# States times W_in for four chunks in one TensorE stretch, and the second softmax's read behind the next scores

## The chip, the cores and the metric

The kernel runs on one core of one Trainium2 chip. The metric is the device time of one execution in microseconds. It uses TensorE (PE) for all products, ScalarE (ACT) and VectorE (DVE) for everything element by element, and SyncE (SP) and ACT for issuing DMAs. GpSimd does almost nothing.

## The reference, cut to what matters

Two computations follow one another: an exchange between 512 tokens and 32 states in each of 8 heads and 8 batches, and a two-layer product with a piecewise quadratic activation on its result.

```python
B, H, S, Ns, D = (8, 8, 512, 32, 64)
scores = scale * np.matmul(x, state.transpose(0, 1, 3, 2))
a = softmax(scores)                        # over the 32 states
xread = np.matmul(a, state)                # tokens read the states
scores2 = scale * np.matmul(state, x.transpose(0, 1, 3, 2))
a2 = softmax(scores2)                      # over the 512 tokens
sread = np.matmul(a2, x)                   # states read the tokens
attn_out = np.concatenate([xread, sread], axis=2)
...
h = x @ w_in                               # x: attn_out as 4352 rows of 512; w_in: 512 x 2048
g = np.where(h >= 1, h, np.where(h <= -1, 0.0, (h + 1) ** 2 / 4))
return g @ w_out                           # w_out: 2048 x 512
```

All data are float32. The weights arrive as float64 and are turned into float32 on the chip.

## The kernel before, in words

**What is computed where.** The product of the attention weights with the states and then with W_in is reordered: for each batch b the states are multiplied with W_in first (`sw`), and the attention weights are multiplied with that. So the first layer is `h = sw^T x attention weights`, in place of `xread` and then `W_in`. W_in is cut into 8 chunks of 256 columns (c = 0 to 7), the hidden layer into 8 steps (j = 0 to 7) of 256 hidden units. Step (b, j) of batch b needs chunk j of `sw` for this batch.

Each float32 operand of the large products is split into a high part and a rest (`ath`/`atl` for the attention weights, `sw_..h`/`sw_..l` for `sw`, `gh`/`gl` for the activation, `wo` for W_out), and a product is three matmuls: high x high, rest x high, high x rest.

**A step (b, j)** does, in the code's order:

- `g1(b, j)`: 12 matmuls of 128x512 (lines 477 to 479), six into each of two banks called h. Then ACT takes Relu of each bank (`relu`, line 482), squares both (`square`, line 485), DVE takes minimum and maximum with the bank itself (`bound`, line 488: two operations, after which the two h banks are free), ACT makes the high part (`high`, line 497), DVE the rest (`low`, line 502).
- `g2` of the step before: 24 matmuls of 128x512 (lines 534 to 536), 8 pairs of three, into four banks called acc. In the last step of a batch they are ordered by output tile, and each finished tile is copied out by ACT (`store`, line 549) and written by a DMA that ACT issues.

So TensorE always has 24 matmuls of the step before to do while ACT and DVE turn h into g.

**Between g1 and g2** of a step stand the small products:

- `sw_make(b, c, 2)` (line 438), in every odd step for the next two steps: 16 matmuls (32 records of two passes each) of 64 rows, 32 columns and 256 elements, eight at a time on different parts of the array (line 417). They write the two banks called mm. ACT copies the high part (line 432), DVE subtracts for the rest (line 436).
- the `Attention` of batch b+1, as a generator of four pieces, one in each even step: `scores` (`sc`, line 253, 8 matmuls of 64 rows and 32 columns) with what the second softmax needs on DVE and ACT; the first softmax and the transposes of the second softmax's weights (`e2p`, line 333); the transposes back, the splitting, and the read `sr` of the second softmax (line 350, 32 matmuls of 128 rows and 32 columns) with its scaling `rs` on DVE (line 358); and the transpose of that read (`rt`, line 364), copied to `srT` by ACT.

`sc`, `e2p`, `sr`, `rt` and `sw` all use the same two mm banks, one after the other.

**What sets the order.** The first batch (b = 0) with all loading and conversion of weights is ordered by a planner (`Plan`) with costs; TensorE's and SP's order there is the written order. Batch 0's phase also holds scores, transposes, read and read's transpose of batch 1. From batch 1 on, the framework's scheduler takes the instructions in the code's order as their priority and moves some of them ahead on their own engine; buffers are tiles in rings, and a tile is free when its last reader is done. The last part, batch index 8, puts the 256 rows of `sread` of all batches through the two layers in four steps.

Of the kernel before, what the change touches and what calls it, by code (L numbers as in the profile page):

```python
# [8 lines left out]
F32 = mybir.dt.float32  # L9
F32R = mybir.dt.float32r  # L10
# [3 lines left out]
ALU = mybir.AluOpType  # L14
# [8 lines left out]
class Plan:  # L23
# [13 lines left out]
    def op(self, key, engine, cost, run, after=(), take=(), ends=()):  # L37

        after = list(after)
        prior = self.last.get(engine) if engine in ("PE", "SP") else None  # L40
        self.last[engine] = key
        self.ops[key] = [engine, cost, run, after, list(take), list(ends), prior]
# [95 lines left out]
def state_exchange_moe(  # L138
# [17 lines left out]
    nc = tc.nc  # L156
    B, P, NT, H, D = x.shape
    S = NT * P
    NS = 32
    DM = H * D  # L160
    NPR = H // 2
    CI = 256
# [3 lines left out]
    NJ = NF // 2  # L166
# [6 lines left out]
    work = ctx.enter_context(tc.tile_pool(name="work", bufs=2))  # L173
# [7 lines left out]
    def ps_h(name):  # L181
        return ps.tile([P, 512], F32, tag="h", bufs=2, name=name)

    def ps_mm(name):
        return ps.tile([P, 2, 512], F32, tag="mm", bufs=1, name=name)
# [3 lines left out]
    half = small.tile([P, 1], F32, name="half")  # L189
# [14 lines left out]
    sb = const.tile([P, B, NPR, NS], F32, name="sb")  # L204
    srT = const.tile([P, NPR, B, NS], F32, name="srT")
    w32 = [const.tile([P, NPR, CI], F32, name=f"w32_{c}") for c in range(NC)]
# [4 lines left out]
    loaded = {}  # L211
    att_of = {}

    def load_xt(b):
        xt = work.tile([P, 2, NPR, S // 2], F32, tag="xt", bufs=1, name=f"xt{b}")
        for i in range(2):
            nc.sync.dma_start(out=xt[:, i], in_=xt_in[b, i])
        return xt
# [6 lines left out]
    class Attention:  # L225
# [116 lines left out]
        def read2(self):  # L342
            b = self.b
            xn = loaded.pop(("xn", b))
            sr = self.sr = ps_mm(f"sr{b}")
            for q in range(2):
                for t in range(NT):
                    for pr in range(NPR):
                        c0 = t * P + pr * NS
                        nc.tensor.matmul(  # L350
                            sr[pr * NS:(pr + 1) * NS, q, :D], lhsT=self.e2[:, q, c0:c0 + NS],
                            rhs=xn[:, t, 2 * pr + q], start=t == 0, stop=t == NT - 1,
                        )

        def scale2(self):
            b = self.b
            self.rs = small.tile([P, 2, D], F32, tag="rs", name=f"rs{b}")
            nc.vector.tensor_tensor(
                out=self.rs, in0=self.sr[:, :, :D], in1=self.r2[:, :, None].broadcast_to([P, 2, D]), op=ALU.mult
            )  # L360

        def keep2(self):
# [7 lines left out]
                out=srT[:, :, self.b], in_=self.rt[:, 0, :P].rearrange("p (g n) -> p g n", n=NS)  # L370
            )

        def steps(self):
            self.scores()
            for q in range(2):
                self.turn(q)
            for q in range(2):
                self.top2(q)
            for q in range(2):
                self.exp2(q)  # L380
            yield
            for f in (self.top1, self.less1, self.exp1, self.sum1, self.inv1, self.norm1):
                for q in range(2):
                    f(q)
            self.turn2()
            self.keep_turned()
            yield
            for q in range(2):
                self.back(q)
                self.high1(q)  # L390
                self.rest(q)
            self.read2()
            self.scale2()
            yield
            self.keep2()
            self.keep()
            yield

    def split_tiles(name):
        hi = work.tile([P, 1024], F32R, tag="wh", name=f"{name}h")
        lo = work.tile([P, 1024], F32R, tag="wl", name=f"{name}l")
        return hi, lo

    chunk = {}
# [27 lines left out]
    def sw_low(b, c):  # L434
        pt, wh, wl = sw_of[b, c]
        nc.vector.tensor_tensor(out=wl, in0=pt, in1=wh.bitcast(F32), op=ALU.subtract)

    def sw_make(b, c, n):
        sw_product(b, c, n)
        sw_high(b, c)  # L440
        sw_low(b, c)

    def wi_split(c):
        wh, wl = (v.rearrange("p (k f) -> p k f", f=CI) for v in split_tiles(f"wj{c}"))
# [59 lines left out]
    def g1(b, j):  # L504
        hid = Hidden(b, j)
        for i in range(2):
            hid.product(i)
            hid.relu(i)
        hid.square()
        for i in range(2):  # L510
            hid.bound(i)
        hid.high()
        hid.low()

    def g2(b, j, half=None):
        n = n_of[b]
        per = S // n
        nt = n // P
        if b not in acc:
            acc[b] = [ps_acc(f"acc{b}_{t}") for t in range(nt)]  # L520
        gh, gl = gs[b, j]
        last = j == NJ // per - 1
        pairs = [(i, t) for i in range(2 * per) for t in range(nt)]
        if last:
            pairs.sort(key=lambda p: p[1])
        if half is not None:
            pairs = pairs[half * len(pairs) // 2:][:len(pairs) // 2]
        for i, t in pairs:
            f = 2 * per * j + i
            oh, ol = wo[f // 2][:, 0, f % 2], wo[f // 2][:, 1, f % 2]  # L530
            c0 = (i % per) * n + t * P
            lh, ll = (v[:, i // per, c0:c0 + P] for v in (gh, gl))
            a = acc[b][t]
            nc.tensor.matmul(a, lhsT=lh, rhs=oh, start=f == 0, stop=False)  # L534
            nc.tensor.matmul(a, lhsT=lh, rhs=ol, start=False, stop=False)  # L535
            nc.tensor.matmul(a, lhsT=ll, rhs=oh, start=False, stop=f == NF - 1)  # L536
            if last and i == 2 * per - 1:
                store(b, t)
# [74 lines left out]
    op = plan.op  # L613
# [25 lines left out]
    atts = {}  # L639
# [34 lines left out]
    def att_ops2(b):  # L674
        def m(name, *a):
            return lambda: getattr(atts[b], name)(*a)

        for q in range(2):
            k = (b, q)
            take = [("tmp" if b == 0 else "e2", ("e2", b))] if q == 0 else []  # L680
            op(("top2",) + k, "DVE", 0.8, m("top2", q), [("sc", b) if b else ("sc", b, 1)] + [("top2", b, 0)] * q, take=take)
            op(("exp2",) + k, "ACT", 0.66, m("exp2", q), [("top2",) + k], ends=[("sc", b)])
        op(("kept", b), "ACT", 0.95, m("keep_turned"), [("e2p", b)], ends=[("e2p", b)])
        op(("rs", b), "DVE", 0.25, m("scale2"), [("sr", b)], ends=[("sr", b)])
        op(("srT", b), "ACT", 0.3, m("keep"), [("rt", b)], ends=[("rt", b)])

    hid = {}

# [12 lines left out]
    def tensor(key, cost, f, after=(), take=(), ends=()):  # L701
        op(key, "PE", cost, f, after, take, ends)
# [24 lines left out]

    def g2_ops(b, j, half):
        k = (b, j)
        tensor(("g2", half) + k, 2.75, lambda: g2(b, j, half), [("gh",) + k, ("gl",) + k, ("wol", j), ("sc done", 0)],  # L730
               ends=[("g",) + k])


# [21 lines left out]
    for side in range(2):  # L755
        tensor(("sc", 0, side), 0.6, lambda side=side: att_start(0, side), [("dma", "xt", 0, side)],
               ends=[("xt", 0)])
# [6 lines left out]
                          take=[("mm", ("e2p", 0))]),  # L764
# [3 lines left out]
                          take=[("mm", ("sc", 1))], ends=[("xt", 1)]),  # L768
        3: lambda: tensor(("rt", 0), 0.3, lambda: atts[0].keep2(), [("rs", 0)], take=[("mm", ("rt", 0))]),
        4: lambda: tensor(("e2p", 1), 0.9, lambda: atts[1].turn2(), [("exp2", 1, 0), ("exp2", 1, 1)],  # L770
                          take=[("mm", ("e2p", 1))]),
        5: lambda: tensor(("sr", 1), 1.1, lambda: atts[1].read2(), [("kept", 1), ("dma", "xn", 1)],
                          take=[("mm", ("sr", 1))], ends=[("e2", 1), ("xn", 1)]),
        6: lambda: tensor(("rt", 1), 0.3, lambda: atts[1].keep2(), [("rs", 1)], take=[("mm", ("rt", 1))]),
    }
    for j in range(NJ):
        g1_ops(0, j)
# [18 lines left out]

    steps = [(b, j) for b in range(1, B + 1) for j in range(NJ if b < B else NJ // 2)]

    def prepare(b, j):
        if b < B:  # L800
            if j % 2 == 0:
                sw_make(b, j, 2)
        elif b == B:
            for c in (2 * j, 2 * j + 1):
                wi_split(c)

    for i, (b, j) in enumerate(steps):
        if j == 0:
            if b + 1 < B:
                loaded["xt", b + 1] = load_xt(b + 1)  # L810
                loaded["xn", b + 1] = load_xn(b + 1)
                att = Attention(b + 1).steps()
            elif b == B:
                sh, sl = (work.tile([P, NPR, B * NS], F32R, tag=t, name=f"s{t}") for t in ("ath", "atl"))
                src = srT.rearrange("p a b n -> p a (b n)")
                nc.vector.tensor_copy(sh, src)
                nc.vector.tensor_tensor(out=sl, in0=src, in1=sh.bitcast(F32), op=ALU.subtract)
                att_of[B] = (sh, sl)
        g1(b, j)
        if i + 1 < len(steps):  # L820
            prepare(*steps[i + 1])
        if b < B and j % 2 == 0:
            next(att, None)
        g2(*(steps[i - 1] if i else (0, NJ - 1)))
    g2(*steps[-1])


# [41 lines left out]
```

## Time and profile before

| what | value |
| --- | --- |
| median of 3 runs | 663.71 us (663.57 to 663.91) |
| span of the profiled execution, first to last instruction | 662.2 us |
| TensorE busy | 653.9 us, 4442 matmul records |
| VectorE busy | 340.3 us |
| ScalarE busy | 356.5 us |
| DMA | 43.65 MB, mean 66 GB/s |

The profile shows one execution by its span, the time between its first and last instruction; the device time of the same kernel is the median above, 1.5 us more than that span. In a timeline each row gives the start in us from the span's start, the duration, the engine, the line of the kernel, the operation, the tile written and those read, their shapes, how many instructions are merged in the row, and in brackets the idle time of the engine before it with what ended it. PE is TensorE's matmuls, PEld its weight loads. Matmuls overlap: a row's duration is not the time after which the next one starts, so on TensorE the distance between starts is what counts.

### The profile page before, as it was taken

The numbers are of one execution on the slowest core, as the hardware profiler recorded it, in microseconds if no ns is written. First come the engines' busy times: TensorE is split into PE (matmuls) and PEld (weight loads), VectorE is DVE, ScalarE is ACT, GpSimd is POOL, SyncE is SP. The second block draws the span as 40 slices with busy tenths as digits, with TensorE's granted clock in tenths as the row PEclk, the third lists the DMA queues.
The fourth block names the chain that finished last, engine by engine and source line by source line (L and its number), as shares of the span: only waits on it lengthen the run. The fifth ranks groups of instructions, "written<-read, shape, count | busy, mean of one in ns | idle before, by whom it ended". The sixth has DMA issues, their size and how long they took to land.

```text
span 662.2 us, 10304 instructions
## 1 busy us (share of the span) xinstructions
PE 653.9 (99%) x4442; PEld 514.2 (78%) x4442; DVE 340.3 (51%) x490; ACT 356.5 (54%) x462; POOL 0.8 (0%) x7
## 2 busy tenths in 40 slices
PE   8999999999999999999999999999999999999997
PEld 6677777777787777777787777777778777778896
DVE  5999947623673239433563338433563343333431
ACT  4899847544554446544554447444653454454642
POOL 0000000000000000000000000000000000000000
PEclk9999999999999999999999999999999999999999
DMA  8986103010301003010301002010100000000101
GB/s 359 400 359 249 64 10 119 0 65 0 120 10 64 1 4 124 0 65 0 128 1 64 1 24 105 0 65 0 65 1 1 1 33 32 1 1 1 63 1 33
DMA packets 11085, 43.65 MB, mean 66 GB/s; under 512 B 1312, under 2 KB 1440, under 8 KB 7968
## 3 DMA queue, kind: packets, MB, share of 16 engines
q1 hardware_dynamic: 6096, 34.28, 13.6%
q10 hardware_dynamic: 4944, 8.72, 3.5%
q8 instruction: 35, 0.57, 0.3%
q14 instruction: 10, 0.08, 0.0%
HBM read 34.08 MB, written 8.91 MB: 65 GB/s over the span
## 4 chain that ended last, share of the span: by engine, by line
PE 91%; ACT 5%; DVE 3%; issue 0%; DMA 0%; POOL 0%; SPq 0%; ACTq 0%; POOLq 0%
PE acc L534 19%; PE acc L536 18%; PE acc L535 18%; PE h L477 9%; PE h L479 9%; PE h L478 9%; PE sw L417 5%; PE sc L253 1%; PE sr L350 1%; PE e2p L333 1%; PE warmed L198 1%; ACT u L482 1%; ACT u L485 1%; ACT raw_i L588 1%; DVE w L596 1%; ACT wo L603 0%
## 5 line engine op out<-in xcount | busy, mean ns | idle before, releaser
L534 PE MATMUL acc<-wo,gh 128*128 128x512 f32 x544 | 218.8, 402 | 0.0
L535 PE MATMUL acc<-wo,gh 128*128 128x512 f32 x544 | 212.3, 390 | 0.0
L536 PE MATMUL acc<-wo,gl 128*128 128x512 f32 x544 | 212.2, 390 | 0.0
L482 ACT ACTIVATE u<-h,half 128x512 f32<-128x512 f32 x136 | 93.7, 693 | 219.9 <-PE h L479 202.6
L488 DVE SCALAR_TENSOR_TENSOR u<-u,h 128x512 f32<-128x512 f32 x136 | 87.0, 680 | 206.7 <-ACT u L485 206.7
L534 PEld LDWEIGHTS acc<-wo,gh 128*128 128x128 f32 x544 | 102.1, 188 | 40.1 <-ACT u L482 12.8
L536 PEld LDWEIGHTS acc<-wo,gl 128*128 128x128 f32 x544 | 102.1, 188 | 22.5 <-issue 0.4
L535 PEld LDWEIGHTS acc<-wo,gh 128*128 128x128 f32 x544 | 102.2, 188 | 19.4 <-DVE wo L607 0.3
L502 DVE TENSOR_TENSOR gl<-u,gh 128x1024 fp32r<-128x1024 f32 x68 | 83.2, 1224 | 33.0 <-ACT gh L497 32.0
L497 ACT CAST gh<-u 128x1024 fp32r<-128x1024 f32 x68 | 71.8, 1056 | 50.3 <-DVE u L488 49.9
L485 ACT ACTIVATE u<-u 128x1024 f32<-128x1024 f32 x68 | 72.5, 1065 | 1.3
L417 PE MATMUL sw<-w,sb 64*32 64x256 f32 x1024 | 36.0, 383 | 1.8 <-DVE w L596 1.3
L417 PEld LDWEIGHTS sw<-w,sb 64*32 64x32 f32 x1024 | 15.1, 106 | 17.9 <-issue 8.8
L479 PE MATMUL h<-atl,sw_0h 128*128 128x512 f32 x60 | 23.6, 393 | 0.3 <-DVE atl L306 0.2
L477 PE MATMUL h<-ath,sw_0h 128*128 128x512 f32 x60 | 23.5, 394 | 0.0
L549 ACT COPY o<-acc 128x512 f32<-128x512 f32 x33 | 18.6, 586 | 9.1 <-PE acc L536 9.0
L478 PE MATMUL h<-ath,sw_0l 128*128 128x512 f32 x60 | 23.5, 391 | 0.0
L479 PE MATMUL h<-atl,sw_6h 128*128 128x512 f32 x60 | 23.4, 389 | 0.0
L479 PE MATMUL h<-atl,sw_2h 128*128 128x512 f32 x60 | 23.4, 389 | 0.0
L477 PE MATMUL h<-ath,sw_2h 128*128 128x512 f32 x60 | 23.3, 389 | 0.0
L478 PE MATMUL h<-ath,sw_2l 128*128 128x512 f32 x60 | 23.3, 389 | 0.0
L477 PE MATMUL h<-ath,sw_4h 128*128 128x512 f32 x60 | 23.3, 389 | 0.0
(174 smaller groups left out, 735.0 us busy)
## 6 DMA issues: line engine op xcount, KB each, us to landing
xt<-in_xt_dram SPq DMA_DIRECT2D x16, 512.0 KB, 4.5
raw_i<-in_moe_w_in_dram SPq DMA_DIRECT2D x8, 1024.0 KB, 6.9
raw_o<-in_moe_w_out_dram SPq DMA_DIRECT2D x8, 1024.0 KB, 9.4
xn<-in_x_dram SPq DMA_DIRECT2D x8, 1024.0 KB, 6.4
out_dram<-o ACTq DMA_DIRECT2D x32, 256.0 KB, 2.0
sb<-in_state_dram SPq DMA_DIRECT2D x1, 448.0 KB, 12.6
out_dram<-o SPq DMA_DIRECT2D x4, 64.0 KB, 1.7
out_dram<-o ACTq DMA_DIRECT2D x4, 64.0 KB, 2.0
```

Of the source, the lines that this page charges most:

```text
L417: nc.tensor.matmul(pt[pr * NS:(pr + 1) * NS, hh, i * CI:(i + 1) * CI], lhsT=sb[rows, b, pr], rhs=w32[c + i][rows, pr], start=True, stop=True,)
L477: nc.tensor.matmul(o, lhsT=wh[:, k, sl], rhs=ah[:, k], start=first, stop=False)
L478: nc.tensor.matmul(o, lhsT=wl[:, k, sl], rhs=ah[:, k], start=False, stop=False)
L479: nc.tensor.matmul(o, lhsT=wh[:, k, sl], rhs=al[:, k], start=False, stop=last)
L482: nc.scalar.activation(out=self.u[:, i], in_=self.hs[i], func=AF.Relu, scale=0.5, bias=half)
L485: nc.scalar.activation(out=self.u, in_=self.u, func=AF.Square)
L488: nc.vector.scalar_tensor_tensor(out=self.u[:, i], in0=self.u[:, i], scalar=1.0, in1=self.hs[i], op0=ALU.min, op1=ALU.max,)
L497: nc.scalar.copy(out=gh, in_=self.u)
L502: nc.vector.tensor_tensor(out=gl, in0=self.u, in1=gh.bitcast(F32), op=ALU.subtract)
L534: nc.tensor.matmul(a, lhsT=lh, rhs=oh, start=f == 0, stop=False)
L535: nc.tensor.matmul(a, lhsT=lh, rhs=ol, start=False, stop=False)
L536: nc.tensor.matmul(a, lhsT=ll, rhs=oh, start=False, stop=f == NF - 1)
```

## The change

It has three parts, all in the part after batch 0 but for one row of the first table.

1. **`sw_four`.** In step 3 of a batch the chunks 4 to 7 of `sw`, and in step 7 the chunks 0 to 3 of the next batch, are made in one stretch of 32 matmuls. The first two chunks go into the two h banks (`own`), the other two into the mm banks (`both`). ACT and DVE split the h banks one by one (512 elements each) and the mm banks together (1024). Batch 1 takes its chunks 0 to 3 in pairs as before, the second pair now in step 1.
2. **The read.** `sr` of batch b is no longer done in step 4 of the batch before, but in step 0 of batch b, right behind the scores of batch b+1, and it writes an h bank in place of the mm banks. `rt` follows in step 1. The read and its transpose of batch 1 leave the table of the first phase for these steps. The load of `xn` for the next batch is written after the read.
3. **The place.** All small products of a step now stand after five of the eight pairs of g2 (15 of 24 matmuls), not between g1 and g2.

```diff
         def read2(self):
             b = self.b
             xn = loaded.pop(("xn", b))
-            sr = self.sr = ps_mm(f"sr{b}")
+            sr = ps_h(f"sr{b}") if b else ps_mm(f"sr{b}")[:, 0]
+            sr = self.sr = sr[:, :2 * D].rearrange("p (q d) -> p q d", q=2)
...
+    def sw_four(b, c):
+
+        pairs = [split_tiles(f"sw{b}_{c + 2 * p}") for p in range(2)]
+        wh, wl = ([v.rearrange("p (q f) -> p q f", q=2) for v in w] for w in zip(*pairs))
+        own = [ps_h(f"sw{b}_{c}_{hh}") for hh in range(2)]
+        both = ps_mm(f"sw{b}_{c + 2}")
+        for i in range(4):
+            cols = slice(i % 2 * CI, (i % 2 + 1) * CI)
+            for pr in range(NPR):
+                for hh in range(2):
+                    rows = slice(hh * 64, hh * 64 + 64)
+                    o = both[:, hh] if i > 1 else own[hh]
+                    nc.tensor.matmul(
+                        o[pr * NS:(pr + 1) * NS, cols], lhsT=sb[rows, b, pr], rhs=w32[c + i][rows, pr],
+                        start=True, stop=True,
+                    )
+            chunk[b, c + i] = wh[i // 2][:, :, cols], wl[i // 2][:, :, cols]
+        for hh in range(2):
+            h, lo = wh[0][:, hh], wl[0][:, hh]
+            nc.scalar.copy(out=h, in_=own[hh])
+            nc.vector.tensor_tensor(out=lo, in0=own[hh], in1=h.bitcast(F32), op=ALU.subtract)
+        nc.scalar.copy(out=wh[1], in_=both)
+        nc.vector.tensor_tensor(out=wl[1], in0=both, in1=wh[1].bitcast(F32), op=ALU.subtract)
...
-        5: lambda: tensor(("sr", 1), 1.1, lambda: atts[1].read2(), [("kept", 1), ("dma", "xn", 1)],
-                          take=[("mm", ("sr", 1))], ends=[("e2", 1), ("xn", 1)]),
-        6: lambda: tensor(("rt", 1), 0.3, lambda: atts[1].keep2(), [("rs", 1)], take=[("mm", ("rt", 1))]),
...
-        g1(b, j)
-        if i + 1 < len(steps):
-            prepare(*steps[i + 1])
-        if b < B and j % 2 == 0:
-            next(att, None)
-        g2(*(steps[i - 1] if i else (0, NJ - 1)))
+        cut = 5
+        g2(*before, (0, cut))
+        if j == 0:
+            if b + 1 < B:
+                atts[b + 1] = Attention(b + 1)
+                atts[b + 1].scores()
+            atts[b].read2()
+            atts[b].scale2()
+            if b + 1 < B:
+                loaded["xn", b + 1] = load_xn(b + 1)
+                atts[b + 1].second()
+        elif j == 1:
+            atts[b].keep2()
+            atts[b].keep()
+            if b == 1:
+                sw_make(b, 2, 2)
+        elif j == 2 and b + 1 < B:
+            atts[b + 1].first()
+        elif j == 3:
+            sw_four(b, 4)
+        elif j == 4 and b + 1 < B:
+            atts[b + 1].halves()
+        elif j == NJ - 1 and b + 1 < B:
+            sw_four(b + 1, 0)
+        g2(*before, (cut, 8))
```

`second`, `first` and `halves` are the pieces of the old generator without the read and its transpose. `g2` takes a range of its eight pairs.

How this moves instructions is seen best at three places. In the rows a name's number tells tiles of the same kind apart, and the brackets hold the engines that a wait is for.

TensorE in step 3 of batch 2, before: `sw` of chunks 4 and 5 between the last matmul of g1 (h) and g2 (acc).

```order
L479 MATMUL h_3_1_1795<-atl_974,sw_2h 128x512
L417 MATMUL sw_4_1810<-w_4_91,sb 32x256 [waits Activation_49]
L417 MATMUL sw_4_1810<-w_4_91,sb 32x256 x7
L417 MATMUL sw_4_1810<-w_5_92,sb 32x256 x8
L534 MATMUL acc_0_1683<-wo_480,gh_2_1731 128x512 [waits Activation_49]
```

The same place with the change, behind 15 matmuls of g2: the last of these, the stretch's first matmuls into the two h banks (`sw_4_0`, `sw_4_1`), the change to the mm banks (`sw_6`), and g2 again.

```order
L555 MATMUL acc_0_1686<-wo_480,gl_2_1738 128x512
L451 MATMUL sw_4_0_1835<-w_4_91,sb 32x256 [waits DVE_49]
L451 MATMUL sw_4_1_1836<-w_4_91,sb 32x256 [waits DVE_49]
...
L451 MATMUL sw_6_1837<-w_6_93,sb 32x256 [waits Activation_49]
L451 MATMUL sw_6_1837<-w_6_93,sb 32x256 x7
L451 MATMUL sw_6_1837<-w_7_94,sb 32x256 x8
L553 MATMUL acc_1_1687<-wo_480,gh_2_1737 128x512
```

Two stretches of two chunks, two steps apart, have become one of four, and its first two matmuls wait for DVE, which reads the h banks last.

TensorE in step 0 of batch 2, before (scores of batch 3 between g1 and g2; the read stood four steps later):

```order
L479 MATMUL h_0_1_1567<-atl_974,sw_0h 128x512
L253 MATMUL sc_1582<-xt_1551,sb 32x512 [waits DMAHW6_49,DMAHW4_49,PE_49]
L253 MATMUL sc_1582<-xt_1551,sb 32x512 x7
L534 MATMUL acc_0_1100<-wo_815,gh_7_1502 128x512 [waits Activation_49]
L535 MATMUL acc_0_1100<-wo_815,gh_7_1502 128x512
```

And with the change:

```order
L555 MATMUL acc_2_1078<-wo_781,gl_7_1468 128x512
L253 MATMUL sc_1589<-xt_1540,sb 32x512 [waits DMAHW4_49,DMAHW0_49,DVE_49]
L253 MATMUL sc_1589<-xt_1540,sb 32x512 x7
L351 MATMUL sr_1601<-xn_1026,e_2_1030 32x64 [waits DMAHW5_49,DVE_49]
L351 MATMUL sr_1601<-xn_1026,e_2_1030 32x64 x31
L553 MATMUL acc_2_1078<-wo_781,gh_7_1467 128x512
```

The read of batch 2 (`sr`) now follows the scores of batch 3 (`sc`) without a large matmul between them.

DVE from step 1 to step 2 of batch 1 with the change (`u_1` are the two bounds of step 1, `gl_1` the rest of its activation, `s_2`, `z` and `zt` the first softmax of batch 2, `sw_2l` the rest of chunks 2 and 3, which TensorE reads in step 2):

```order
L508 SCALAR_TENSOR_TENSOR u_1_1052<-u_1_1052,h_1_0_1053 128x512 [waits Activation_49]
L508 SCALAR_TENSOR_TENSOR u_1_1052<-u_1_1052,h_1_1_1061 128x512
L284 TENSOR_REDUCE s_2_982<-z_980 128x16 [waits Activation_49]
L293 TENSOR_TENSOR z_980<-z_980,s_2_982 128x512 [waits DVE_49]
L522 TENSOR_TENSOR gl_1_1073<-u_1_1052,gh_1_1072 128x1024 [waits PE_49,Activation_49]
L288 TENSOR_SCALAR s_2_982<-s_2_982 128x16 [waits DVE_49]
L300 STREAM_TRANSPOSE zt_1335<-z_980 128x512 [waits DVE_49]
L432 TENSOR_TENSOR sw_2l<-sw_2_1098,sw_2h 128x1024 [waits Activation_49]
```

Before, `sw_2l` stood right behind the two bounds of step 1; now `gl_1` and a piece of the softmax stand ahead of it.

More of the change, by code (lines that the diff above doesn't have):

```diff
@@ L350, in read2 @@
                         nc.tensor.matmul(
-                            sr[pr * NS:(pr + 1) * NS, q, :D], lhsT=self.e2[:, q, c0:c0 + NS],
+                            sr[pr * NS:(pr + 1) * NS, q], lhsT=self.e2[:, q, c0:c0 + NS],
                             rhs=xn[:, t, 2 * pr + q], start=t == 0, stop=t == NT - 1,
@@ L358, in scale2 @@
             nc.vector.tensor_tensor(
-                out=self.rs, in0=self.sr[:, :, :D], in1=self.r2[:, :, None].broadcast_to([P, 2, D]), op=ALU.mult
+                out=self.rs, in0=self.sr, in1=self.r2[:, :, None].broadcast_to([P, 2, D]), op=ALU.mult
             )
@@ L371, in keep, with second @@
             )
-        def steps(self):
-            self.scores()
+        def second(self):
             for q in range(2):
@@ L380, in steps, with first @@
                 self.exp2(q)
-            yield
+        def first(self):
             for f in (self.top1, self.less1, self.exp1, self.sum1, self.inv1, self.norm1):
@@ L386, in steps, with halves @@
             self.keep_turned()
-            yield
+        def halves(self):
             for q in range(2):
@@ L391, in steps @@
                 self.rest(q)
[L392 to L397, printed above, removed]
     def split_tiles(name):
@@ L513, in g1, with g2 @@
         hid.low()
-    def g2(b, j, half=None):
+    def g2(b, j, part=(0, 8)):
         n = n_of[b]
@@ L525, in g2 @@
             pairs.sort(key=lambda p: p[1])
-        if half is not None:
-            pairs = pairs[half * len(pairs) // 2:][:len(pairs) // 2]
+        pairs = pairs[part[0]:part[1]]
         for i, t in pairs:
@@ L683, in att_ops2 @@
         op(("kept", b), "ACT", 0.95, m("keep_turned"), [("e2p", b)], ends=[("e2p", b)])
-        op(("rs", b), "DVE", 0.25, m("scale2"), [("sr", b)], ends=[("sr", b)])
-        op(("srT", b), "ACT", 0.3, m("keep"), [("rt", b)], ends=[("rt", b)])
+        if b == 0:
+            op(("rs", b), "DVE", 0.25, m("scale2"), [("sr", b)], ends=[("sr", b)])
+            op(("srT", b), "ACT", 0.3, m("keep"), [("rt", b)], ends=[("rt", b)])
     hid = {}
@@ L729, in g2_ops @@
         k = (b, j)
-        tensor(("g2", half) + k, 2.75, lambda: g2(b, j, half), [("gh",) + k, ("gl",) + k, ("wol", j), ("sc done", 0)],
+        tensor(("g2", half) + k, 2.75, lambda: g2(b, j, (4 * half, 4 * half + 4)), [("gh",) + k, ("gl",) + k, ("wol", j), ("sc done", 0)],
                ends=[("g",) + k])
@@ L797, in state_exchange_moe @@
     steps = [(b, j) for b in range(1, B + 1) for j in range(NJ if b < B else NJ // 2)]
[L799 to L804, printed above, removed]
-                wi_split(c)
-    for i, (b, j) in enumerate(steps):
+    for i, (b, j) in enumerate(steps):
+        if (b, j) == (B, 0):
+            sh, sl = (work.tile([P, NPR, B * NS], F32R, tag=t, name=f"s{t}") for t in ("ath", "atl"))
+            src = srT.rearrange("p a b n -> p a (b n)")
+            nc.vector.tensor_copy(sh, src)
+            nc.vector.tensor_tensor(out=sl, in0=src, in1=sh.bitcast(F32), op=ALU.subtract)
+            att_of[B] = (sh, sl)
+        if b + 1 < B and j == 0:
+            loaded["xt", b + 1] = load_xt(b + 1)
+        g1(b, j)
+        if i + 1 < len(steps) and steps[i + 1][0] == B:
+            for c in (2 * steps[i + 1][1], 2 * steps[i + 1][1] + 1):
+                wi_split(c)
+        before = steps[i - 1] if i else (0, NJ - 1)
+        if b == B:
+            g2(*before)
+            continue
+        cut = 5
+        g2(*before, (0, cut))
@@ L808, in state_exchange_moe @@
         if j == 0:
             if b + 1 < B:
-                loaded["xt", b + 1] = load_xt(b + 1)
-                loaded["xn", b + 1] = load_xn(b + 1)
[L812 to L818, printed above, removed]
```

## The prediction

> **What bounds the kernel now.** I read the page first: the busy shares, the granted clock and the chain of work that ended last.
>
> ```profile
> span 662.2 us, 10304 instructions
> PE 653.9 (99%) x4442; PEld 514.2 (78%) x4442; DVE 340.3 (51%) x490; ACT 356.5 (54%) x462; POOL 0.8 (0%) x7
> PEclk9999999999999999999999999999999999999999
> PE 91%; ACT 5%; DVE 3%; issue 0%; DMA 0%; POOL 0%; SPq 0%; ACTq 0%; POOLq 0%
> ```
>
> TensorE sets the end at the full clock; ACT and DVE are half idle. A change helps only if TensorE has less to do or waits less, and it hurts if a new wait reaches TensorE. The number of matmuls stays the same here, so the question is what TensorE loses between them. The timeline of TensorE answers it. A stretch of large matmuls:
>
> ```profile
> 307.57 0.39 PE L477 MATMUL h<-ath,sw_6h 128*128 128x512 f32 x1
> 310.06 0.39 PE L479 MATMUL h<-atl,sw_6h 128*128 128x512 f32 x1
> ```
>
> Eleven starts in 2.49 us: one each 0.2266 us (the 0.39 overlaps the next). Without anything between, the third start after a given one comes 0.68 us later. Now the stretches of small matmuls: the states-times-W_in product (sw) of one chunk, of two chunks, the scores (sc), and the second read (sr), each with the large matmul ahead of it and three behind.
>
> ```profile
> 39.26 0.39 PE L479 MATMUL h<-atl,sw_2h 128*128 128x512 f32 x1
> 39.58 0.66 PE L417 MATMUL sw<-w,sb 64*32 64x256 f32 x16
> 40.17 0.50 PE L534 MATMUL acc<-wo,gh 128*128 128x512 f32 x1
> 40.74 0.40 PE L536 MATMUL acc<-wo,gl 128*128 128x512 f32 x1
> ...
> 93.85 0.39 PE L536 MATMUL acc<-wo,gl 128*128 128x512 f32 x1
> 94.17 1.09 PE L417 MATMUL sw<-w,sb 64*32 64x256 f32 x32
> 95.20 0.50 PE L534 MATMUL acc<-wo,gh 128*128 128x512 f32 x1
> 95.77 0.39 PE L536 MATMUL acc<-wo,gl 128*128 128x512 f32 x1
> ...
> 319.47 0.39 PE L479 MATMUL h<-atl,sw_0h 128*128 128x512 f32 x1
> 319.79 1.09 PE L253 MATMUL sc<-xt,sb 64*32 64x512 f32 x16
> 320.81 0.50 PE L534 MATMUL acc<-wo,gh 128*128 128x512 f32 x1
> 321.14 0.39 PE L535 MATMUL acc<-wo,gh 128*128 128x512 f32 x1
> 321.37 0.40 PE L536 MATMUL acc<-wo,gl 128*128 128x512 f32 x1
> ...
> 356.77 0.39 PE L479 MATMUL h<-atl,sw_4h 128*128 128x512 f32 x1
> 357.08 1.10 PE L350 MATMUL sr<-xn,e 128*32 128x64 f32 x64
> 358.12 0.50 PE L534 MATMUL acc<-wo,gh 128*128 128x512 f32 x1
> 358.69 0.39 PE L536 MATMUL acc<-wo,gl 128*128 128x512 f32 x1
> ```
>
> Start of the third matmul behind, less start of the one ahead, less 0.68: sw of one chunk 0.80 us, of two 1.24, sc 1.22, sr 1.24. One more chunk costs 0.44, so a stretch of sw costs 0.80 - 0.44 = **0.36 us for being a stretch**, whatever is in it (2 x 0.80 - 1.24 says the same). The sc rows show where: 0.32 into the stretch against 0.23 (0.09 lost), 0.33 from the first large start behind to the second (0.11), and about 0.15 inside (the two-chunk body of 1.03 is that much short of twice the one-chunk body, 0.59). The sw stretch here stands between acc matmuls, the one-chunk one behind h, so the place does not matter.
>
> **The change, part by part.** Of the 27 two-chunk sw stretches in batches 1 to 7, one stays (chunks 2 and 3 of batch 1) and 26 become 13 of four chunks. Each pair that joins loses one fixed part: 13 x 0.36 = **-4.6 us**. A four-chunk stretch then costs 0.36 + 4 x 0.44 = 2.12. It has 64 matmul records; the sr row shows 64 in 1.04 us, so issuing them is not the limit.
>
> The read of batch b now follows the scores of batch b+1, six times (b = 1 to 6; the read of batch 7 stays alone). At most the whole fixed part goes, 0.36. At least 0.09: if going from the 64*32 tiles of sc to the 128*32 tiles of sr costs as much as going back to large matmuls (0.15 + 0.11), only the second entry is saved. I take the middle, 0.22, since no row shows this boundary: 6 x 0.22 = **-1.3 us** (-0.5 to -2.2). The Trainium skill (TensorEngine Tiling (Array Packing), section Tiling Modes, key properties) says that changing the tiling mode, not just the tile, drains TensorE. The 0.09 before each small stretch agrees. It speaks against this half of the change, since sc and sr are different modes and one of four drains is gone, not two: by it alone the term would be near -0.5; without it, -2.2.
>
> The transposes (rt, e2p) and the reads of batch 1 are moved to other steps at the same price.
>
> Where could TensorE now wait? First at the four-chunk stretch, whose first half writes both h banks. These come free when DVE's two "bound" operations of the same step have read them:
>
> ```profile
> 310.49 0.69 ACT L482 ACTIVATE u<-h,half 128x512 f32<-128x512 f32 x1 [0.67 <-PE h L479]
> 311.21 1.06 ACT L485 ACTIVATE u<-u 128x1024 f32<-128x1024 f32 x1
> 312.30 1.29 DVE L488 SCALAR_TENSOR_TENSOR u<-u,h 128x512 f32<-128x512 f32 x2 [4.61 <-ACT u L485]
> 313.67 1.05 ACT L497 CAST gh<-u 128x1024 fp32r<-128x1024 f32 x1 [0.51 <-DVE u L488]
> 62.10 0.68 DVE L436 TENSOR_TENSOR sw_5l<-sw,sw_5h 128x512 fp32r<-128x512 f32 x1
> 62.84 1.09 PE L333 MATMUL e2p<-ident,e 128*128 128x128 f32 x8
> ```
>
> Counted from the last g1 start (310.06): the bounds end at +3.53. The last two rows show DVE's hand-over to TensorE: 62.78 to 62.84, 0.06. So the second bank is free at +3.59. The stretch comes after 15 matmuls of g2, at 15 x 0.2266 + 0.32 = +3.72. **No wait, but only 0.13 us of room.** I take 0.
>
> Then the result: the own banks are done at about +4.75 (half of 2.12 later). ACT is free of gh at +4.66, DVE of gl at about +5.9. With the half-size copy and subtract of the first batch
>
> ```profile
> 80.78 0.59 ACT L432 CAST sw_7h<-sw 128x512 fp32r<-128x512 f32 x1
> 81.41 0.69 DVE L436 TENSOR_TENSOR sw_7l<-sw,sw_7h 128x512 fp32r<-128x512 f32 x1
> ```
>
> the first pair is ready at +6.6, the second at +7.3. The next g1 starts at 25 x 0.2266 + 2.12 = +7.8 and needs the second pair only at its fourth matmul: 1.2 us of room. Behind these on DVE stands the subtract of the other pair, wanted two steps later. The scores start 3.4 us later in their step, and their chain used to take until this row:
>
> ```profile
> 339.95 0.69 DVE L306 TENSOR_TENSOR atl<-zt,ath 128x512 fp32r<-128x512 f32 x1 [0.55 <-ACT ath L303]
> ```
>
> 340.64 - 319.79 = 20.9 after sc began, so now until 3.7 + 20.9 + 0.3 (the scaling of the read, put ahead of it on DVE) = 24.9 after the last g1 of step 0. The bounds of step 3 are wanted at 3 x 8.16 (36 matmuls a step) + 2.2 + 2.2 = 28.9: 4 us of room. The loads have most of a batch to land; on SP the one of xn now waits for the read, behind which only loads for the next batch stand. All this is costed at nothing because TensorE's g2 covers it.
>
> Second, **batch 1**, which still takes its first four chunks in pairs:
>
> ```profile
> 99.97 0.39 PE L479 MATMUL h<-atl,sw_0h 128*128 128x512 f32 x1
> 102.21 1.28 DVE L488 SCALAR_TENSOR_TENSOR u<-u,h 128x512 f32<-128x512 f32 x2 [4.56 <-ACT u L485]
> 103.41 1.31 DVE L260 STREAM_TRANSPOSE z<-sc 128x512 f32<-128x512 f32 x2
> 105.22 1.20 DVE L502 TENSOR_TENSOR gl<-u,gh 128x1024 fp32r<-128x1024 f32 x1
> 107.12 0.69 ACT L322 ACTIVATE e<-sc,nm 128x512 f32<-128x512 f32 x1 [1.47 <-DVE nm L318]
> 110.12 1.07 ACT L485 ACTIVATE u<-u 128x1024 f32<-128x1024 f32 x1
> 112.51 1.22 DVE L436 TENSOR_TENSOR sw_2l<-sw,sw_2h 128x1024 fp32r<-128x1024 f32 x1
> ```
>
> In step 0 of batch 1 only six g2 matmuls stand between g1 and the scores, so sc would start at 99.97 + 6 x 0.2266 + 0.32 = 101.65 and sr at about 102.6; its h bank is free after the first bound, 102.21 + 0.68 + 0.06 = 102.95: **+0.4 us**. In step 1, sw of chunks 2 and 3 is made after g1, not with it. DVE has turns to 104.7, gl to 105.9, rs (0.3), two maxima (1.3): the exponential starts about 107.6, 0.5 later than before. So the square ends at 111.7, the bounds at 113.1, gh (1.05) at 114.2, gl at 115.5, a small operation and a turn (0.9) at 116.4, and then sw_2l, 1.22, at 117.6. TensorE gets to the h matmul that reads sw_2l 30 starts, one sw stretch and rt (1.36) after the last g1 of step 1, which starts at 102.95 + 1.03 + 0.11 + 20 x 0.2266 = 108.6: at 116.8. **+0.8 us** (0 if DVE gains what I added up as rounded; 1.6 if ACT loses as much again).
>
> Sum: -4.6 - 1.3 + 0.4 + 0.8 = **-4.7 us**. Span 662.2 - 4.7 = 657.5. The median of the runs, 663.7, lies 1.5 above the profiled span; with the same 1.5, **659.0 us**. Its own bounds: -0.9 if sc and sr join wholly, -1.2 if batch 1 does not wait, +0.8 on each for the other way: 657.0 to 660.6.
>
> **Rivals.**
>
> (1) The banks of h come late. The room at each four-chunk stretch is 0.13 us. If a stretch waits for x more than that, 13 x is lost. For it: ACT's and DVE's order is tight there. Against it: in step 3 and step 7 nothing of the softmax is left on either engine. With x = 0.15, 2 us are lost: 661.0.
>
> (2) Slower than before: the softmax chain of the next batch runs into step 3, so that TensorE stands at the four-chunk stretch until DVE has done less1, sum1 and norm1 ahead of the bounds. That would hold in six batches. It decides from 0.8 us a batch (4.7 / 6); that is an overrun of 4 + 0.8 us over my count. At 1.2 us it gives 659.0 + 7.2 = 666.2. Against it: the 4 us of room.
>
> (3) The fixed part is not a matter of stretches, and joining saves nothing: 663.7 + 1.2 = 664.9. Against it: 0.80 and 1.24, from two sizes of the same product.
>
> (4) sc and sr join wholly and batch 1 doesn't wait: 659.0 - 0.9 - 1.2 = 656.9.
>
> **How the numbers follow.** The forecast with its bounds has 0.70, (4) and what lies near it 0.10, (1) 0.12, (2) 0.05, (3) 0.03. 0.2% of 663.7 is 1.3 us, about what a measurement of this kernel can tell from no change. Faster by more than that (below 662.4): the forecast, (4), and nearly all of (1): 0.90. Within: the rest of (1) and milder forms of (2) and (3): 0.05. Slower: 0.05. The range with 8 in 10 leaves out the far end of (4) and (2), (3): 656.9 to 661.2.
>
> **What would show it.** In the profile after: 13 stretches of 64 sw records, each 2.1 us by the count above, with 0.32 ahead of them; more there means rival 1 or 2, and the row of DVE's bounds says which (at +3.53, or later). Six stretches of sc and sr of 2.1 to 2.4 together against 2.46. A gap of about 0.4 before sr in batch 1 and about 0.8 in step 2 of batch 1, before the h matmul that reads sw_2l, and no other gap over 0.35. The forecast is wrong if a four-chunk stretch costs 2.4 or more, or if a gap comes back in every batch.

## The result and the profile after

| kernel | median of 5 runs | lowest to highest | profiled span |
| --- | --- | --- | --- |
| before | 663.71 us | 663.50 to 664.04 | 662.2 us |
| after | 658.84 us | 658.29 to 659.15 | 656.8 us |

The ratio after to before is 0.9925, with a 95% interval of 0.9913 to 0.9937: 4.9 us less. The forecast was 659.0.

The page of the kernel after shows the same picture as before, with TensorE at the end of nearly everything:

```profile
span 656.8 us, 10337 instructions
PE 647.7 (99%) x4442; PEld 518.1 (79%) x4442; DVE 340.1 (52%) x503; ACT 359.6 (55%) x475; POOL 0.8 (0%) x7
PE 88%; ACT 6%; DVE 4%; issue 1%; DMA 0%; POOL 0%; ACTq 0%; SPq 0%; POOLq 0%
```

The number of matmul records is the same 4442, and DVE and ACT have 13 more instructions each: the halves of the 13 four-chunk results. TensorE's busy time fell by 6.2 us with no matmul removed, so what went is time that TensorE spent in and around the short stretches. TensorE's timeline after, around one four-chunk stretch and around one stretch of scores and read (same columns as in the prediction):

```profile
202.06 0.39 PE L555 MATMUL acc<-wo,gl 128*128 128x512 f32 x1
202.38 1.96 PE L451 MATMUL sw<-w,sb 64*32 64x256 f32 x64
204.27 0.50 PE L553 MATMUL acc<-wo,gh 128*128 128x512 f32 x1
204.85 0.40 PE L555 MATMUL acc<-wo,gl 128*128 128x512 f32 x1
...
174.24 0.39 PE L555 MATMUL acc<-wo,gl 128*128 128x512 f32 x1
174.56 1.09 PE L253 MATMUL sc<-xt,sb 64*32 64x512 f32 x16
175.58 1.10 PE L351 MATMUL sr<-xn,e 128*32 128x64 f32 x64
176.61 0.50 PE L553 MATMUL acc<-wo,gh 128*128 128x512 f32 x1
177.18 0.39 PE L555 MATMUL acc<-wo,gl 128*128 128x512 f32 x1
```

By the prediction's count (third large start behind, less the one ahead, less 0.68), the four-chunk stretch costs 204.85 - 202.06 - 0.68 = 2.11 us, and scores with read 177.18 - 174.24 - 0.68 = 2.26. I call this the cost of a stretch from here on, and the time from its first start to the next large start its body: 1.89 and 2.05 here.

### The profile page after: what moved, and what is told of

Read it like the earlier page. It is cut to its first block, busy times and chain, and to the rows that moved or that the text cites. A ratio compares the mean times of both kernels' runs of the same rounds, so it can differ in the third digit from the quotient of the medians.

```text
span 656.8 us, 10337 instructions
## 1 busy us (share of the span) xinstructions
PE 647.7 (99%) x4442; PEld 518.1 (79%) x4442; DVE 340.1 (52%) x503; ACT 359.6 (55%) x475; POOL 0.8 (0%) x7
## 4 chain that ended last, share of the span: by engine, by line
PE 88%; ACT 6%; DVE 4%; issue 1%; DMA 0%; POOL 0%; ACTq 0%; SPq 0%; POOLq 0%
PE acc L553 18%; PE acc L554 17%; PE acc L555 17%; PE h L498 9%; PE h L499 9%; PE h L497 9%; PE sw L451 4%; PE sr L351 1%; ACT u L502 1%; PE sc L253 1%; PE e2p L333 1%; PE warmed L198 1%; ACT u L505 1%; ACT e L322 1%; ACT raw_i L607 1%
## 5 line engine op out<-in xcount | busy, mean ns | idle before, releaser
L451 PE MATMUL sw<-w,sb 64*32 64x256 f32 x832 | 25.4, 379 | 0.0
L498 PE MATMUL h<-ath,sw_4l 128*128 128x512 f32 x60 | 23.4, 389 | 0.0
L497 PE MATMUL h<-ath,sw_6h 128*128 128x512 f32 x60 | 23.3, 389 | 0.0
L498 PE MATMUL h<-ath,sw_6l 128*128 128x512 f32 x60 | 23.3, 389 | 0.0
```

The lines of the kernel that those rows point to most:

```text
L451: nc.tensor.matmul(o[pr * NS:(pr + 1) * NS, cols], lhsT=sb[rows, b, pr], rhs=w32[c + i][rows, pr], start=True, stop=True,)
L497: nc.tensor.matmul(o, lhsT=wh[:, k, sl], rhs=ah[:, k], start=first, stop=False)
L498: nc.tensor.matmul(o, lhsT=wl[:, k, sl], rhs=ah[:, k], start=False, stop=False)
```

## The experiments

The theory: a stretch of small matmuls has a fixed price, so joining stretches is the whole gain; nothing waits at the four-chunk stretch; between scores and read a part of the fixed price is paid once more. Its rivals: the gain comes from elsewhere (where the work stands, or less waiting), and the price between scores and read has another cause. Times are to be held against 663.54 us (median of 18 runs of the kernel before, 662.95 to 664.03) for numbers 1, 2, 4 and 7, and against 663.95 (one run) for numbers 3, 5 and 6, which have one run each and are read by their traces.

**1. Cut the four-chunk stretch in two again.** Everything stays where the change put it (banks, split into halves, order), but one pair of g2, three large matmuls, stands between the first two chunks and the last two.

```diff
         for i in range(4):
+            if i == 2 and between:
+                between()
...
-            sw_four(b, 4)
+            sw_four(b, 4, lambda: g2(*before, (5, 6)))
+            cut = 6
```

> The change with each four-chunk stretch cut in two by one pair of g2 (three large matmuls), same step, same banks, same copies. Theory (a stretch of small matmuls has a fixed price of 0.36 us, whatever is in it): each pair of two-chunk stretches costs 2 x 1.24 = 2.47 in place of 2.11, 13 times, so +4.7 us: 663.5 us, nearly the time of the kernel before. Rival (the gain came from the new place behind five pairs of g2, or from the h banks): the two halves together still cost 2.1, and the time stays at 658.8 us.

Measured: 663.74 us (662.81 to 664.45, 10 runs), ratio 1.0001 (0.9992 to 1.0011). TensorE in this kernel:

```profile
203.66 0.39 PE L557 MATMUL acc<-wo,gl 128*128 128x512 f32 x1
203.97 1.09 PE L453 MATMUL sw<-w,sb 64*32 64x256 f32 x32
205.00 0.50 PE L555 MATMUL acc<-wo,gh 128*128 128x512 f32 x1
...
205.57 0.39 PE L557 MATMUL acc<-wo,gl 128*128 128x512 f32 x1
205.89 1.09 PE L453 MATMUL sw<-w,sb 64*32 64x256 f32 x32
206.91 0.50 PE L555 MATMUL acc<-wo,gh 128*128 128x512 f32 x1
```

The two halves cost 1.235 and 1.233 us, as two-chunk stretches did before; together 0.36 more than joined. 13 x 0.36 = 4.7, and the time went up by 4.9; the other 0.2 is a longer wait for `sw_2l` in batch 1 (described in the next section). All of the net gain is gone with this one cut: the rest of the change, the read's join and the waits of batch 1 among it, comes to nothing in sum, within the 0.6 us of the interval.

**2. Start the four-chunk stretch one pair of g2 earlier.** The prediction found 0.13 us of room there. Three large matmuls less in front are 0.68 us.

```diff
-        cut = 5
+        cut = 4 if j in (3, NJ - 1) else 5
```

> The change with the four-chunk stretches of steps 3 and 7 one pair of g2 (three matmuls) earlier. Theory (the second h bank is free 3.59 us after the last start of g1, and the stretch could now start at 12 x 0.2266 + 0.32 = 3.04): TensorE waits 0.55 us inside each of the 13 stretches, +7.1 us: 665.9 us, and the gap stands right behind the stretch's first matmul. Rival (the room was much more than 0.13 us): the stretch costs 2.11 as before and the time stays at 658.8 us.

Measured: 665.31 us (664.46 to 666.23, 9 runs), ratio 1.0028 (1.0018 to 1.0038): slower than the kernel before. TensorE and DVE in this kernel:

```profile
202.01 0.39 PE L555 MATMUL acc<-wo,gl 128*128 128x512 f32 x1
202.33 2.48 PE L451 MATMUL sw<-w,sb 64*32 64x256 f32 x64
204.73 0.50 PE L553 MATMUL acc<-wo,gh 128*128 128x512 f32 x1
...
201.53 1.29 DVE L508 SCALAR_TENSOR_TENSOR u<-u,h 128x512 f32<-128x512 f32 x2 [5.01 <-ACT u L505]
```

The stretch starts at 202.33, but the second h bank is in use until DVE's bounds end at 201.53 + 1.29 = 202.82. The body grows from 1.89 to 2.40 us; the stretch costs 0.51 us more, 13 times, 6.6 us in all (the time rose by 6.5). By the prediction's room it should be 0.68 - 0.13 = 0.55; nine of the stretch's 64 records start before the bounds end, which would account for the 0.04 less. So the place matters, and the room was as small as forecast: one pair earlier and the whole gain is lost.

**3. Start it one pair of g2 later.** If a wait for the banks were hidden in the 2.11 us, this would take it away.

```diff
-        cut = 5
+        cut = 6 if j in (3, NJ - 1) else 5
```

> The change with the four-chunk stretches of steps 3 and 7 one pair of g2 (three matmuls) later. Theory (on the other side there is room too: the first pair of the result is ready at 6.7 us after the last start of g1, the next g1 comes at 7.8 and needs the second pair, ready at 7.4, only at 8.5): stretches of 2.11 us, no gap before g1, 658.8 us. Rival (the result is just in time with five pairs): a gap of about 0.7 before g1 after each stretch, 13 x 0.7 = 9 us more, 668 us.

Measured in one run: 658.81 us, span 657.0; every four-chunk stretch costs 2.107 as before, and no g1 waits for its result. This kernel also shows how to read a line that looks like a wait. In the list of waits, the weight loads of the four-chunk stretch appear in the kernel after as

```profile
PEld sw L451 <- DVE u L508: 4.6, 13, 0.4
```

4.6 us in total, 13 times, 0.4 at the longest: it reads as if DVE's bounds held up each stretch by 0.35 us. With the stretch three large matmuls (0.68 us) later the list says

```profile
PEld sw L451 <- issue: 4.6, 13, 0.4
```

The same 4.6 us, 13 times, now with nothing to wait for, and the stretch starts 0.32 after the large matmul ahead of it in both. These 0.35 are the weight loads' share of changing from large to small matmuls, not a wait. Nor does the list show the real wait of experiment 2, which falls inside the stretch: there the line is again 4.6 us, 13 times, with DVE's name. The label names the semaphore that came last, not what the time is for.

**4. Put a pair of g2 between scores and read.** This undoes the join of the second part alone, except in batch 7, whose read stands alone anyway.

```diff
                 atts[b + 1].scores()
+            if b + 1 < B:
+                g2(*before, (5, 6))
+                cut = 6
             atts[b].read2()
```

> The change with one pair of g2 between the scores and the read. Theory (going from 64*32 to 128*32 tiles costs the part inside a stretch again, so that joining saves only 0.20 each): scores 1.22 and read 1.24 apart, 6 x 0.20 = 1.2 us more, less the 0.29 that batch 1 waits for its h bank now: 659.7 us. Rival (the change of tiles is free and joining saves the whole 0.36): the two cost 2.2 together less, so apart 6 x 0.36 = 2.2 us more, less 0.3: 660.7 us.

Measured: 659.90 us (659.49 to 660.37, 4 runs), ratio 0.9945 (0.9930 to 0.9960). TensorE in this kernel:

```profile
174.67 1.09 PE L253 MATMUL sc<-xt,sb 64*32 64x512 f32 x16
175.69 0.50 PE L553 MATMUL acc<-wo,gh 128*128 128x512 f32 x1
...
176.58 1.10 PE L351 MATMUL sr<-xn,e 128*32 128x64 f32 x64
177.61 0.50 PE L553 MATMUL acc<-wo,gh 128*128 128x512 f32 x1
```

The bodies alone are 1.02 and 1.03 us. Joined they are 2.05 (first section): their sum, to the hundredth. So the join saves what lies outside the bodies, 0.09 at the entry and 0.11 behind, 0.20 a time, and nothing inside. In this kernel a read so soon behind the scores costs 1.26 instead of 1.24, so that the trace makes it 5 x 0.22 = 1.1 us in batches 2 to 6. In batch 1 the pair of g2 also covers a wait of the read (below): there the two cost 2.48 us apart and 2.55 joined, 0.07 gained. The time rose by 1.1. Its interval (about 658.9 to 660.9) holds the rival's 660.7 too; it is the bodies in the trace that decide.

**5. The read ahead of the scores.** If the part paid again lay in going from 64*32 to 128*32 tiles in this order, or in the bank that the read writes, the other order would change it.

```diff
         if j == 0:
+            atts[b].read2()
             if b + 1 < B:
                 atts[b + 1] = Attention(b + 1)
                 atts[b + 1].scores()
-            atts[b].read2()
             atts[b].scale2()
```

> The change with the read ahead of the scores (in batch 1 the read stands after two of the eight score matmuls). Theory (the part inside a stretch is paid at each change of tiles, whichever way): from the first small matmul to the first large one 2.05 us again, the sum of the two alone (1.02 + 1.03), and 658.8 us. Rival (only going from 64*32 to 128*32 costs, or the order of the two products matters otherwise): less than 1.95, which saves 6 x 0.15 = 0.9 us: 657.9 us; or more than 2.15.

```profile
176.20 1.10 PE L351 MATMUL sr<-xn,e 128*32 128x64 f32 x64
177.23 1.09 PE L253 MATMUL sc<-xt,sb 64*32 64x512 f32 x16
178.25 0.50 PE L553 MATMUL acc<-wo,gh 128*128 128x512 f32 x1
```

The body is 178.25 - 176.20 = 2.05 us again, in each of batches 2 to 6: the order does not matter. The time of this run, 661.22, is well above the theory's, and its span, 658.5, is 1.7 above that of the kernel after. The trace says why: the read of batch 1 now needs its h bank about 1 us sooner, and the body there is 3.34 instead of 2.33; the wait for `sw_2l` is 0.2 longer, and the first phase took 0.4 more in this execution. The rest of the longer time, 0.7 us, lies outside the span and is not explained. The time alone would have misled.

**6. Eight unused small matmuls ahead of the scores.** In each of the six joined stretches the kernel does one more chunk of the states-times-W_in product into two h banks; nobody reads it. It has the scores' tiles, 64*32, but another moving operand, another length (256) and other banks. The theory says that only the tile's mode costs, so this adds its own 0.43 and no fixed part; the rival says that any change of product costs.

```diff
+                spare = [ps_h(f"spare{b}_{hh}") for hh in range(2)]
+                for pr in range(NPR):
+                    for hh in range(2):
+                        rows = slice(hh * 64, hh * 64 + 64)
+                        nc.tensor.matmul(
+                            spare[hh][pr * NS:(pr + 1) * NS, :CI], lhsT=sb[rows, b, pr], rhs=w32[0][rows, pr],
+                            start=True, stop=True,
+                        )
                 atts[b + 1].scores()
```

> The change with eight more matmuls of the states-times-W_in kind (one chunk, result unused, into the two h banks) ahead of the scores of steps 0 of batches 1 to 6: another product, other operands and another length (256 in place of 512 elements), but the same 64*32 tiles as the scores. Theory (it is the change of tiles that costs, not that of the product): the stretch grows by one chunk's 0.43 alone, from 2.05 to 2.48 us: 6 x 0.43 = 2.6 us more, 661.4 us. Rival (each change of product costs the part inside a stretch): 2.05 + 0.43 + 0.16 = 2.64, 662.4 us.

```profile
176.42 0.66 PE L842 MATMUL spare<-w,sb 64*32 64x256 f32 x16
176.88 1.06 PE L253 MATMUL sc<-xt,sb 64*32 64x512 f32 x16
177.87 1.10 PE L351 MATMUL sr<-xn,e 128*32 128x64 f32 x64
178.90 0.50 PE L553 MATMUL acc<-wo,gh 128*128 128x512 f32 x1
```

The body is 2.48 us in batches 2 to 6, 0.43 more than without. The theory holds in the trace. The time of the one run, 662.66, is the rival's number, but not for the rival's reason: in batch 1 the added chunk waits for its h banks, and the body there is 4.38 us, against 2.33 in the kernel after; with the spare chunk's 0.43 alone it would be 2.76. Five times 0.43 and these 2.05 make 4.2, less 0.2 by which the wait for `sw_2l` is shorter; the span is 4.1 us longer (660.9).

**7. Take the waits of batch 1 away.** Two waits in batch 1 were in the forecast, and the trace of the kernel after has both (rows in the next section). This version makes chunks 2 and 3 of batch 1 right behind g1 of step 1 rather than in the middle of g2, moves the transpose of batch 1's read to step 5, and lets the scores of batch 1's step 0 start one pair later.

```diff
         g1(b, j)
+        if (b, j) == (1, 1):
+            sw_make(b, 2, 2)
...
-        cut = 5
+        cut = 6 if (b, j) == (1, 0) else 5
...
-        elif j == 1:
+        elif j == (5 if b == 1 else 1):
             atts[b].keep2()
             atts[b].keep()
-            if b == 1:
-                sw_make(b, 2, 2)
```

> The change with batch 1 mended: its second pair of chunks right behind g1 of step 1, the transpose of its read in step 5, and its scores and read after six pairs of g2. Theory (batch 1 loses 0.29 at the read's h bank and 0.50 at the h matmul that reads the rest of chunks 2 and 3): both gaps go, 658.8 - 0.8 = 658.0 us. Rival (what TensorE does not wait for there it waits for in the next steps): 658.8 us, with gaps of the same sum elsewhere in batch 1.

Measured: 657.62 us (657.28 to 658.37, 4 runs), ratio 0.9912 (0.9897 to 0.9927). Scores and read of batch 1:

```profile
99.80 1.09 PE L253 MATMUL sc<-xt,sb 64*32 64x512 f32 x16
100.81 1.10 PE L351 MATMUL sr<-xn,e 128*32 128x64 f32 x64
101.84 0.50 PE L553 MATMUL acc<-wo,gh 128*128 128x512 f32 x1
```

The body is 2.05 (2.04 by these rounded rows) and the stretch costs 2.26, as in the other batches; the g1 that reads `sw_2l` no longer waits. In the trace 0.79 us of waiting is gone. It is the fastest version, but its interval overlaps with that of the change: that it is faster is shown by the trace's two waits, not by the times alone. The waits have not come back elsewhere, as the rival has it: from the first states-times-W_in stretch of batch 1 to the end, this execution is 0.86 us shorter. The other 0.45 us by which its span is shorter lie ahead of that, in the first phase, which this version leaves as it is.

## Why the prediction was right

The terms of the sum, with what the trace of the kernel after shows for each:

| term | predicted | measured |
| --- | --- | --- |
| 13 joins of the states-times-W_in product | -4.6 (four-chunk stretch 2.12) | -4.7 (2.107 each) |
| 6 joins of scores and read | -1.3 (bounds -0.5 to -2.2) | -1.2 (0.20 each) |
| the read waits in batch 1 | +0.4 | +0.3 |
| g1 waits for `sw_2l` in batch 1 | +0.8 | +0.5 |
| wait at the four-chunk stretches | 0 (room 0.13) | 0 |
| time outside the span | 1.5 | 2.0 |

**The fixed price of a stretch** held, and experiment 1 shows that it is the whole net gain. Rival 3, that joining saves nothing, falls with it.

**The room at the four-chunk stretch.** The end of the bounds and the start of the stretch, the two times that make the room, held to the hundredth. TensorE and DVE of step 3 of batch 2, after:

```profile
198.66 0.39 PE L499 MATMUL h<-atl,sw_2h 128*128 128x512 f32 x1
...
200.90 1.29 DVE L508 SCALAR_TENSOR_TENSOR u<-u,h 128x512 f32<-128x512 f32 x2 [5.01 <-ACT u L505]
...
204.50 1.28 DVE L459 TENSOR_TENSOR sw_4l<-sw,sw_4h 128x512 fp32r<-128x512 f32 x2
...
206.47 0.40 PE L497 MATMUL h<-ath,sw_4h 128*128 128x512 f32 x1
```

From the last g1 start, 198.66, the bounds end at +3.53 (predicted +3.53), the stretch starts at 202.38, +3.72 (predicted +3.72), the second half of the own banks' result is ready at 204.50 + 1.28, +7.1 (predicted +7.3), and the next g1 starts at +7.8 (predicted +7.8). Rival 1 (late banks) did not come, and experiment 2 shows what it would have cost. Rival 2 (the softmax chain in the way) did not come either: the bounds' idle time of 5.01 us in front of them says that DVE had long been free, and all 13 stretches cost 2.11. Rival 4, the whole join and no wait in batch 1, failed on both.

**Scores and read.** The middle between the bounds, 0.22, stood for two unknowns: whether the price inside and the price behind the first part are paid again at the change from 64*32 to 128*32 tiles. One is and one is not. The 0.15 inside is paid in full (experiment 4: 2.05 = 1.02 + 1.03; experiment 5: in either order). The 0.11 behind is not, since it belongs to the large matmuls behind a stretch. So the middle was nearly right by luck, because one of two parts fell each way.

The sums of bodies alone would also fit a read that has no part inside, with a change of tiles that costs nothing. The single records rule that out. The last eight records of the scores, ahead of the read in the kernel after and ahead of a large matmul in experiment 5:

```profile
175.01 0.64 PE L253 MATMUL sc<-xt,sb 64*32 64x512 f32 x8
175.58 0.24 PE L351 MATMUL sr<-xn,e 128*32 128x64 f32 x1
...
177.69 0.64 PE L253 MATMUL sc<-xt,sb 64*32 64x512 f32 x8
178.25 0.50 PE L553 MATMUL acc<-wo,gh 128*128 128x512 f32 x1
```

What follows starts 0.57 us after these eight in both, so leaving the scores' tiles costs the same whichever tiles come next. Likewise the read's last four records start 0.17 us ahead of what follows, a large matmul or the scores, where its groups of four otherwise follow each other after 0.06.

Experiment 6 and the four-chunk stretch show that a change of product, length or bank inside one kind of tile costs nothing: two bodies of 1.024 joined give 2.05 - 0.16 = 1.89, and the spare chunk adds 0.43.

The Trainium skill (TensorEngine Tiling (Array Packing), section Tiling Modes, key properties) says that a change of the mode drains TensorE and a change of the tile in one mode does not. These runs agree: 0.14 to 0.16 us inside for each mode, 0 where the mode stays. The -0.5 that I drew from it was too small a gain, since I had counted the 0.11 of the next large matmul with the drain.

**Batch 1** is where the working was off, by 0.4 of 1.2 us. The read's wait, after:

```profile
99.56 1.09 PE L253 MATMUL sc<-xt,sb 64*32 64x512 f32 x16
100.87 1.10 PE L351 MATMUL sr<-xn,e 128*32 128x64 f32 x64 [0.21 <-DVE u L508]
101.90 0.50 PE L553 MATMUL acc<-wo,gh 128*128 128x512 f32 x1
...
100.12 1.28 DVE L508 SCALAR_TENSOR_TENSOR u<-u,h 128x512 f32<-128x512 f32 x2 [4.56 <-ACT u L505]
```

The body is 2.33 (2.34 by these rounded rows), 0.29 more than in the other batches, where 0.4 was predicted. It waits for DVE's first bound as described. The second wait, after:

```profile
106.61 0.39 PE L499 MATMUL h<-atl,sw_0h 128*128 128x512 f32 x1
...
109.70 1.22 DVE L508 SCALAR_TENSOR_TENSOR u<-u,h 128x512 f32<-128x512 f32 x2
...
112.08 1.23 DVE L522 TENSOR_TENSOR gl<-u,gh 128x1024 fp32r<-128x1024 f32 x1
...
113.30 0.71 DVE L300 STREAM_TRANSPOSE zt<-z 128x512 f32<-128x512 f32 x1
113.93 1.19 DVE L432 TENSOR_TENSOR sw_2l<-sw,sw_2h 128x1024 fp32r<-128x1024 f32 x1
...
114.56 0.39 PE L555 MATMUL acc<-wo,gl 128*128 128x512 f32 x1
115.17 0.50 PE L498 MATMUL h<-ath,sw_2l 128*128 128x512 f32 x1 [0.23 <-DVE sw_2l L432]
115.51 0.40 PE L499 MATMUL h<-atl,sw_2h 128*128 128x512 f32 x1
```

Counted from the last g1 start of step 1 (106.61; 108.6 in the prediction), TensorE came to the matmul at 114.56 + 0.23, +8.2, as predicted. DVE was earlier than I had added up: bounds end at +4.3 (predicted +4.5), `gl` at +6.7 (+6.9), the small operation and the turn behind it took 0.6 and not 0.9, and `sw_2l` was ready at +8.5, not +9.0. So the wait was 0.4 and not 0.8; 0.1 more went in the matmul behind it. The step that was off is the chain of DVE's durations in that paragraph: I summed rounded full durations, while the rows here start before the one ahead has ended (the turn `zt` ends at 114.01, `sw_2l` starts at 113.93). That is 0.3 of the 0.5 us; the other 0.2 had come about before the bounds ended and is not traced further.

**What the sum owes to chance.** The span fell by 5.4 us, where the terms measured give 4.7 + 1.2 - 0.3 - 0.5 = 5.1 less. The first phase, of which the change takes out only the read and its transpose, was 0.66 us shorter in the profiled execution after up to where that read stood, and as much so already 8 us after the start; the cause is not traced. Over the eight profiled executions that share this phase (the kernel after and its seven variants) its end varies by 1.1 us, so I count the 0.66 as chance. Some 0.3 us came back at the end. And the time outside the span was 2.0 us in the profiled execution (1.8 to 2.0 in all five), not the 1.5 that I took from the median of the runs less the span of another execution. These differences have opposite signs and nearly cancel: the forecast is closer, at 0.2 us, than its terms are. Two smaller points of the working: the count of a stretch stops at the third large start behind it, and up to the ninth a stretch costs 0.01 to 0.04 us more, which makes the two joins 4.6 and 1.4 in place of 4.7 and 1.2; and the lower of the forecast's own bounds adds up to 656.9, not 657.0.

## What to carry to other kernels

Where TensorE sets the end, look at the distances between starts and not at busy shares: here a stretch of small matmuls between large ones had a price that did not depend on its length (about 0.36 us in stretches of one, two and four chunks), and it can be read from two sizes of the same product. Join stretches that have the same tile shape first, since only these save all of it, and check in a timeline when each bank that the longer stretch writes comes free: three large matmuls decided between 4.9 us gained and 1.8 lost. When a list of waits names an engine, move the work a little later and see whether the waiting time stays: if it does, it is not that engine.

## What the runs showed of the hardware that I had not expected

- The fixed price of a stretch (0.36 us) has three parts that come apart. 0.16 us is inside the bodies: it comes once for each kind of small tile in a stretch (2.05 for two kinds, 1.89 for four chunks of one kind). Most of it is paid on leaving the tiles: in a four-chunk stretch the groups of eight records follow each other after 0.22 us, and the large matmul comes 0.35 after the last group.
- The 0.11 us behind a stretch does not need a small matmul at all: after the plain wait for `sw_2l`, the second large matmul also came 0.34 us after the first (115.17 to 115.51), and not 0.23. In both cases the weight loads were no longer ahead: the first large matmul's load starts together with it and the next one 0.11 us later (115.17 and 115.28 here), where in a row of large matmuls a load starts 0.22 us before its matmul. That this is the cause is not shown.
- The 0.09 us at the entry is not there for small matmuls with the large ones' tiles. The transposes of batch 2 have 128*128 tiles and start 0.23 us after the large matmul ahead, the normal distance:

```profile
192.99 0.39 PE L555 MATMUL acc<-wo,gl 128*128 128x512 f32 x1
193.22 1.03 PE L333 MATMUL e2p<-ident,e 128*128 128x128 f32 x8
```
